# A long convolution followed by phase mixing: first weight loads gated, late operand loads pinned ahead, operand copies split between two issuing engines, PSUM banks reordered

## The chip, the cores and the metric

The kernel runs on one core of one Trainium2 chip. The metric is the device time of one execution in microseconds, and medians over several executions are quoted. The kernel before had run three times when the prediction was written: median 2134.66 us (2131.06 to 2136.18).

## The reference, cut to what matters

```python
def _attn_ref(x, h):                       # x: (8, 5696, 128), h: (5696, 128)
    L = 2 * S
    Yf = np.fft.rfft(x, n=L, axis=1) * np.fft.rfft(h, n=L, axis=0)[None]
    return np.fft.irfft(Yf, n=L, axis=1)[:, :S, :]

def _moe_ref(x, w_theta, w_tok_r, w_tok_i, w_ch):   # x is the result above
    theta = x @ w_theta
    zr, zi = x * np.cos(theta), x * np.sin(theta)
    y = einsum('ts,bsd->btd', w_tok_r, zr) + einsum('ts,bsd->btd', w_tok_i, zi)
    u = x + y
    return u + np.maximum(u @ w_ch, 0.0)
```

A long convolution comes first. Then each token's value is turned by a phase ("phases"), and two 5696 x 5696 matrices W mix the tokens. The mixing is nearly all of the work.

## The kernel before

The convolution runs in stages a to d. Its last stages make `yt` (channels on partitions). A phase step takes one tile of 128 tokens: PE transposes it, PE makes theta, ACT makes sine and cosine, and DVE multiplies (the "zz products"). 22 steps for the first half of the columns ("first series") are woven into stages c and d. 22 for the second half ("second series") are woven into the first products with W. The results must end up, in another layout, in eleven operand tiles b0 to b10. For some tiles they go by "direct copies" from the product in SBUF straight into the b tile. For b9 and b10 (the "late" ones) they go through HBM (`z_hbm`).

The direct copies in the phase step, where some go to Pool (GpSimd) and the rest to SP (SyncE):

```python
            zz = (fh.tile([P, 2, HD * CK], F16, tag="hs", name="zz").bitcast(BF16) if k < 4 else
                  sides["phases"]["zz"].tile([P, 2, 512], BF16, tag="zz", name="zz"))
            zr, zi = zz[:, 0], zz[:, 1]
        ...
        zi_eng.tensor_mul(zi, red, yflat)
        nc.vector.tensor_mul(zr, mag, yflat)
        ...
            if tags is None and j in home:
                for r in range(2):
                    (nc.gpsimd if r and (e or zz_n[0] % 2) else nc.sync).dma_start(
                        home[j][32 * i:32 * i + 32, :4096]...[:, :, q_, r],
                        zz[e * 64 + r:e * 64 + 64:2])
            elif tags is None:
                nc.sync.dma_start(z_hbm[:, p_, j, q_, i].rearrange("z t n -> t z n"), zz[rows])
```

The W loads go into a ring of six slots, four DMAs of 32 partitions to a slot, all issued by Pool. `pump` issues as many as the ring and the limit `upto` allow. `open_ring` starts it:

```python
    def load_w(a, row0, p, j0, nj, ng=4):
        n = ring["n"] % 6
        ring["n"] += 1
        wb = ring["all"][:, n * WB // 6:(n + 1) * WB // 6].rearrange("p (g j) -> p g j", g=4)
        for i in range(4):
            nc.gpsimd.dma_start(
                wb[32 * i:32 * i + 32, :ng, :nj * 64],
                bass.AP(tensor=a.tensor, ...))
        return wb
```

The second series and the first visit to W are woven like this (`i == 1` is the second stretch; `product` is two matmuls of line 974):

```python
        if i == 1:
            for q, (h, s) in enumerate(((0, 0), (0, 1), (1, 0), (1, 1))):
                for n in range(4):
                    for j in range(TJ):
                        product((held, a)[s], s * TJ + j, j, n, (h,))
                        if (n * TJ + j) % 2:
                            next_steps(1)          # one phase step of the second series
                    if n % 2 and q == 1:
                        ring["upto"] += 1
                        pump()
                    if q == 3 and n == 0:
                        ring["upto"] = len(queue)
                        nxt = prepare(2)
            continue
```

The late operands, their loads, the last rows of `ya` (input of the second series), and the first background phases, which load `yT` and `yy` on SP as well:

```python
    def load_b(p, j, pool, eng=nc.scalar):
        t_ = tile_b(p, j, pool)
        for z in range(2):
            eng.dma_start(t_[...], z_hbm[z, p, j]...)
    ...
    def load_ya1(yt=None):
        ...
            for e in range(2):
                nc.sync.dma_start(st[1][HD:, 2 + e, :],
                                  yt[64 * e:64 * e + 64].rearrange("p m n -> p (m n)")[:, :H])
    ...
        if (p, tt, j0 + s0) == (0, 1, 0):
            spread[0][0]()
            spread[1][0]()
    ...
        if first_of_pair:
            ms = [mps.tile([P, 512], F32, tag=f"m{q}", name=f"m{q}") for q in (... (M3, M5, M1, M7))]
```

## Time and profile before

| | before |
|---|---|
| median of three executions | 2134.66 us |
| profiled span | 2137.7 us |
| first matmul of the last stage c (line 323) | 402.4 us |
| first transpose of the second series | 459.5 us |
| last theta of the second series | 515.5 us |
| end of the first visit to W | 546.1 us |
| end of the second visit | 585.6 us |

The last five rows are landmarks read from the timeline of PE. They cut the stretch that the change touches into stages. The prediction below shows the lines of the page that say where the time goes. Two more views are needed later. The first is Pool's timeline at the end of the second series (start, length, engine, line, what it wrote from what, count, and in brackets the idle time before and what ended it):

```profile
512.04 1.10 POOL L436 DMA_DIRECT2D b<-zz  x2 [1.86 <-DVE zz L423]
513.13 1.66 POOL L498 DMA_DIRECT2D ring<-in_moe_w_tok_r_dram  x3
514.75 2.18 POOL L498 DMA_DIRECT2D ring<-in_moe_w_tok_i_dram  x4
516.89 0.61 POOL L572 DMA_DIRECT2D y_hbm<-ring  x1
518.95 0.55 POOL L436 DMA_DIRECT2D b<-zz  x1 [1.45 <-DVE zz L423]
```

The second is the view of SP's waits between 500 and 535 us (total, times, longest):

```profile
SPq L730 <- ACT ring L729: 6.3, 1, 6.3
```

This is the store of a background phase that holds SP's queue for 6.3 us, with the loads of b9 and b10 behind it.

### The profile page before, as it was taken

How to read it: one execution, taken by the hardware profiler on the slowest of the kernel's cores; microseconds unless marked ns; L12 is line 12 of the kernel's file. 1: busy time of each engine (PE TensorE's matmuls, PEld its weight loads, DVE VectorE, ACT ScalarE, POOL GpSimd, SP SyncE). 2: the span in 40 equal slices, each digit the busy share in tenths (PEclk: the TensorE clock that was granted, in tenths of full speed). 3: DMA queues.
4: the chain of work that ended last, by engine and by line, in shares of the span. 5: the costliest groups of instructions: out<-in, count | busy, mean ns of one | idle time of the engine just before them, and what ended most of it. 6: DMA issues, size and time to landing. Idle time of an engine off the chain costs nothing.

```text
span 2137.7 us, 41292 instructions
## 1 busy us (share of the span) xinstructions
PE 1996.2 (93%) x15586; PEld 1123.7 (53%) x15765; DVE 1594.6 (75%) x2880; ACT 675.3 (32%) x997; POOL 898.5 (42%) x1643
## 2 busy tenths in 40 slices
PE   4788889778999999999999998999999999999998
PEld 3787888654444444444444443444444444444444
DVE  7767767677678888888886757577776768686867
ACT  5777877785223333233310000011111111111111
POOL 5301010227345545454557543444545454545451
PEclk8688889899999999999999999999999999999999
DMA  7357474889889998998999879687879797969794
GB/s 145 96 126 169 120 171 112 224 245 230 168 147 180 172 187 157 177 172 178 174 174 153 148 133 277 101 143 131 154 128 158 126 156 127 157 122 159 127 153 90
DMA packets 408839, 334.95 MB, mean 157 GB/s; under 512 B 85927, under 2 KB 359207, under 8 KB 407655
## 3 DMA queue, kind: packets, MB, share of 16 engines
q0 software_dynamic: 225568, 155.93, 51.9%
q1 hardware_dynamic: 177088, 164.84, 27.0%
q10 hardware_dynamic: 5984, 11.54, 1.5%
q8 instruction: 123, 2.02, 0.4%
q14 instruction: 76, 0.62, 0.1%
HBM read 377.11 MB, written 92.49 MB: 220 GB/s over the span
## 4 chain that ended last, share of the span: by engine, by line
PE 64%; DVE 3%; DMA 3%; issue 1%; POOL 1%; ACT 0%; DVEq 0%; ACTq 0%
PE m L1052 57%; PE m L974 2%; DMA b<-z_hbm 2%; DVE c L1059 1%; PE v L786 1%; PE utp L779 1%; PE m L1056 1%; DVE wt L699 1%; PE m L931 1%; POOL ring L498 1%; PE m L929 1%; PE theta_ps L388 0%; PE tpz L727 0%; DMA yT<-yt_hbm 0%; DMA wl<-in_moe_w_tok_i_dram 0%
## 5 line engine op out<-in xcount | busy, mean ns | idle before, releaser
L498 POOL DMA_DIRECT2D ring<-in_moe_w_tok_i_dram x720 | 388.0, 547 | 691.1 <-DVE wt L699 613.4
L498 POOL DMA_DIRECT2D ring<-in_moe_w_tok_r_dram x720 | 386.9, 547 | 151.4 <-DVE wt L699 87.5
L699 DVE STREAM_TRANSPOSE wt<-ring 128x384 f32<-128x384 f32 (+2 forms) x720 | 360.3, 528 | 113.9 <-PE m L1052 70.4
L1052 PE MATMUL m<-b,wt 128*128 128x512 bf16 x1598 | 383.8, 379 | 4.2 <-DVE wt L699 1.7
L1052 PEld LDWEIGHTS <-wt 128*128 128x128 bf16 x1804 | 176.1, 98 | 215.8 <-DVE wt L699 4.4
L1059 DVE TENSOR_TENSOR c<-c,m 128x512 f32<-128x512 f32 x412 | 267.4, 676 | 0.4 <-PE m L1052 0.4
L781 ACT ACTIVATE ring<-utp 128x512 bf16<-128x512 bf16 (+1 forms) x86 | 50.9, 592 | 608.7 <-PE utp L779 608.7
L323 PE MATMUL ps<-r_u,u_t 128*128 128x128 f16 x1024 | 132.8, 229 | 14.1 <-DVE u_t L307 12.6
L324 PE MATMUL ps<-r_v,v_t 128*128 128x128 f16 x1024 | 131.9, 229 | 0.1
L974 PE MATMUL m<-b,wt 128*128 128x512 bf16 x469 | 112.8, 386 | 12.2 <-DMA b<-zz 5.8
L776 ACT ACTIVATE ub<-c 128x512 bf16<-128x512 f32 (+1 forms) x90 | 56.3, 628 | 198.9 <-DVE c L945 117.3
L129 POOL DMA_DIRECT2D x<-in_x_dram x64 | 33.9, 536 | 193.8 <-PE ps L193 181.6
L323 PEld LDWEIGHTS <-u_t 128*128 128x128 f16 x1024 | 106.6, 104 | 15.7 <-DVE u_t L307 15.7
L324 PEld LDWEIGHTS <-v_t 128*128 128x128 f16 x1024 | 105.7, 103 | 2.7 <-DVE v_t L307 1.3
L307 DVE TENSOR_TENSOR u_t<-xs,hs 128x1024 f16<-128x1024 f16 x96 | 71.1, 741 | 38.9 <-ACT xs L305 23.8
L305 ACT ACTIVATE xs<-ps 128x1024 f16<-128x1024 f32 x96 | 94.6, 1014 | 15.3 <-DVE v_t L307 8.8
L193 PE MATMUL ps<-f_t,x 89*128 89x180 f16 x512 | 82.1, 316 | 9.7 <-ACT xs L305 7.5
L974 PEld LDWEIGHTS <-wt 128*128 128x128 bf16 x528 | 51.2, 100 | 67.0 <-issue 12.7
L211 PEld LDWEIGHTS <-w_t 64*128 64x128 f16 x3240 | 63.6, 105 | 37.2 <-issue 23.1
L193 PEld LDWEIGHTS <-x 89*128 89x128 f16 x512 | 73.5, 232 | 12.0 <-issue 11.3
L390 ACT ACTIVATE red<-theta_ps,magic 128x512 f32<-128x512 f32 (+1 forms) x46 | 31.6, 687 | 135.9 <-PE theta_ps L388 105.1
L729 ACT ACTIVATE ring<-tpz 128x512 bf16<-128x512 bf16 (+1 forms) x46 | 27.4, 597 | 144.1 <-PE tpz L727 126.9
(2888 smaller groups left out, 3867.2 us busy)
## 6 DMA issues: line engine op xcount, KB each, us to landing
ring<-in_moe_w_tok_r_dram POOLq DMA_DIRECT2D x352, 96.0 KB, 4.6
ring<-in_moe_w_tok_i_dram POOLq DMA_DIRECT2D x352, 96.0 KB, 4.9
ring<-in_moe_w_tok_r_dram POOLq DMA_DIRECT2D x352, 80.0 KB, 4.5
ring<-in_moe_w_tok_i_dram POOLq DMA_DIRECT2D x352, 80.0 KB, 3.8
hs<-hf_hbm SPq DMA_DIRECT2D x192, 128.0 KB, 3.2
cp_hbm<-c SPq DMA_DIRECT2D x88, 256.0 KB, 2.5
c<-cp_hbm SPq DMA_DIRECT2D x88, 256.0 KB, 4.5
out_dram<-c SPq DMA_DIRECT2D x88, 256.0 KB, 4.2
```

Of the source, the lines that this page charges most:

```text
L193: nc.tensor.matmul(ps[:, i // 2, (i % 2) * 2 * K1:(i % 2 + 1) * 2 * K1], lhs(q + i), f1_t[:NB], start=True, stop=True)
L211: nc.tensor.matmul(ps[:, e, j * HD:(j + 1) * HD], w_t2[rows, c0 + j, N2 * (1 - ri):N2 * (3 - ri)], a_st["a"][rows, ri * K1 + c0 + j, :], s ...
L305: nc.scalar.activation(xs[:, :, :, :ck], ps, AF.Copy)
L307: nc.vector.tensor_tensor(uv[r][:, :, :, c0:c0 + ck], xs[:, :, :, :ck], hv[:, r:r + 1, :, :ck].to_broadcast([P, 2, HD, ck]), op=mult)
L323: nc.tensor.matmul(o, u_t[:, at:at + P], r_u, start=True, stop=False)
L324: nc.tensor.matmul(o, v_t[:, at:at + P], r_v, start=False, stop=True)
L498: nc.gpsimd.dma_start(wb[32 * i:32 * i + 32, :ng, :nj * 64], bass.AP(tensor=a.tensor, offset=a.offset + row0 * S + p * H + i * QR + j0 * 6 ...
L699: nc.vector.transpose(wt.rearrange("p j t r -> p (j t r)").bitcast(F32).rearrange("p (j g t) -> p g j t", j=TJ, g=4)[:, :ng, :nj], wb[:, : ...
L776: nc.scalar.activation(ub[:m].rearrange("p b d -> p (b d)"), c[:m], AF.Copy)
L974: nc.tensor.matmul(ms[n // 2 * 2 + h], a[n][:, j, :, r], bts_of[p][jj][n % 2 * 2 + h][:, r, :], start=(n % 2 == 0 and jj == 0 and r == 0), ...
L1052: nc.tensor.matmul(ms[q], a[q][:, j, :, r], bts[jj][q][:, r, :], start=(jj == 0 and r == 0), stop=(jj == NJ - 1 and r == 1 and q not in left))
L1059: nc.vector.tensor_tensor(c, z, ms[q], op=op)
```

## The change

It has four parts, each with its own intent. (1) Each of the first six W slots is first touched by a one-element Pool copy that reads a zz product, so that the W loads wait until the phases are under way and don't compete with the last loads of `h`. (2) The four PSUM banks of the first products are taken before the first steps of the second series, so that those steps fall on the oldest convolution banks. (3) Every second direct copy goes to Pool: SP has 36 instead of 48, Pool 36 instead of 24. (4) The background loads on SP are put after the loads of b9 and b10.

```diff
@@ phase step
             zr, zi = zz[:, 0], zz[:, 1]
+            sides["zz"] = zz
...
-                    (nc.gpsimd if r and (e or zz_n[0] % 2) else nc.sync).dma_start(
+                    (nc.gpsimd if r else nc.sync).dma_start(
@@ load_w
+        if ring["n"] <= 6:
+            nc.gpsimd.tensor_copy(wb[0:1, 0, 0:1], sides["zz"][0:1, 0, 0:1])
         for i in range(4):
             nc.gpsimd.dma_start(
@@ load_b
-            eng.dma_start(
+            sides["late"] = eng.dma_start(
@@ main loop
                 nxt = prepare(0)
+                ms = [mps.tile([P, 512], F32, tag=f"m{q}", name=f"m{q}") for q in (M3, M5, M1, M7)]
                 next_steps(2)
         if (p, tt, j0 + s0) == (0, 1, 0):
-            spread[0][0]()
-            spread[1][0]()
+            with tc.issue_after(sides["late"].ins):
+                spread[0][0]()
+                spread[1][0]()
...                      (ms is no longer taken here for the first pair; and the addends and
                          first phases of the first two visits stand in the same issue_after)
```

More of the change, by code (lines that the diff above doesn't have):

```diff
@@ L948 @@
         classic = plain(p, tt)
+        if first_of_pair and i:
+            ms = [mps.tile([P, 512], F32, tag=f"m{q}", name=f"m{q}") for q in (range(7) if not classic else (M7, M5, M1, M3) if p else (M2, M6, M1, M7))]
         if first_of_pair:
-            ms = [mps.tile([P, 512], F32, tag=f"m{q}", name=f"m{q}") for q in (range(7) if not classic else (M7, M5, M1, M3) if p else (M2, M6, M1, M7) if tt else (M3, M5, M1, M7))]
             where = ((tt, 1), (22 + tt, 0), (tt, 0), (22 + tt, 1))
@@ L956 @@
         if j0 + s0 == (3 if classic else 2) * TJ:
-            cs = [addend(p, n, t, h) for n, (t, h) in enumerate(where)]
+            with tc.issue_after(sides["late"].ins) if p == 0 and tt == 0 else ExitStack():
+                cs = [addend(p, n, t, h) for n, (t, h) in enumerate(where)]
         def aside(first_of, second_of):
@@ L963, in aside @@
                 _, first, second = spread.pop(0)
-                first()
-                if len(spread) > 1:
-                    spread[1][0]()
+                with tc.issue_after(sides["late"].ins) if p == 0 and tt == 1 else ExitStack():
+                    first()
+                    if len(spread) > 1:
+                        spread[1][0]()
             if second_of and second is not None:
```

## The prediction

> **What bounds the kernel now.** I read the page first: busy time by engine, then the 40 slices. They separate a start that is not bound by PE from a long rest that is.
>
> ```profile
> PE 1996.2 (93%) x15586; PEld 1123.7 (53%) x15765; DVE 1594.6 (75%) x2880; ACT 675.3 (32%) x997; POOL 898.5 (42%) x1643
> ...
> PE   4788889778999999999999998999999999999998
> ...
> PEclk8688889899999999999999999999999999999999
> ```
>
> PE is short of 90% in slices 1 to 10 only (53 us each; to about 550 us). The table by stretch puts numbers on it: busy us of PE, PEld, DVE, ACT, POOL, then granted clock, DMA share and GB/s.
>
> ```profile
> 395.00:400.00 5.00, 0.00 (x0) 0.00 (x0) 1.72 (x3) 1.46 (x3) 3.97 (x8) 0.50 0.98 183
> ...
> 482.00:513.00 31.00, 25.09 (x226) 15.76 (x228) 24.61 (x46) 23.76 (x40) 23.68 (x44) 1.00 0.97 251
> ...
> 529.00:541.00 12.00, 6.89 (x27) 2.96 (x26) 8.12 (x15) 0.83 (x2) 3.75 (x7) 0.72 1.04 270
> ...
> 800.00:900.00 100.00, 99.26 (x504) 46.94 (x513) 83.59 (x164) 33.58 (x54) 51.46 (x96) 1.00 0.93 169
> ```
>
> After 550 us PE is over 99% busy at full clock, and nothing there can be gained by moving loads. The change acts between 390 and 545 us, where convolution ends, the phases run and the first matmuls with W start. So I listed PE's waits in 380 to 560 us (total, times, longest) and found each in the timeline of PE (start, length, idle before it and what ended it).
>
> ```profile
> PE ps L323 <- DVE u_t L307: 7.5, 1, 7.5
> PE m L974 <- DMA b<-zz: 5.8, 3, 3.5
> PE m L974 <- DMA b<-z_hbm: 5.3, 2, 4.9
> PE tpz L566 <- ACT red L411: 3.8, 1, 3.8
> ...
> PE tpz L566 <- DVE ring L571: 2.1, 2, 1.6
> PE tpz L566 <- DMA ya<-yt: 1.6, 1, 1.6
> ```
> ```profile
> 402.41 0.29 PE L323 MATMUL ps<-r_u,u_t 128*128 128x128 f16 x1 [7.50 <-DVE u_t L307]
> ...
> 459.45 0.48 PE L566 MATMUL tpz<-ident_bf,ya 128*128 128x128 bf16 x3 [3.76 <-ACT red L411]
> 461.56 0.29 PE L566 MATMUL tpz<-ident_bf,ya 128*128 128x128 bf16 x1 [1.64 <-DMA ya<-yt]
> ...
> 494.15 0.82 PE L974 MATMUL m<-b,wt 128*128 128x512 bf16 x2 [1.32 <-DMA b<-zz]
> ...
> 513.24 0.42 PE L974 MATMUL m<-b,wt 128*128 128x512 bf16 x1 [3.54 <-DMA b<-zz]
> ...
> 536.70 1.01 PE L974 MATMUL m<-b,wt 128*128 128x512 bf16 x2 [4.89 <-DMA b<-z_hbm]
> ```
>
> The six add up to 26 us. PE runs at half clock after four of them (5.1 us after 402.4, 4.6 after 461.5, 2.7 after 513.2, 3.3 after 536.7: half of that, 8 us, is lost). So 34 us, 1.6% of 2134.66, is the ceiling, and a gain over 2% is nearly excluded from the start.
>
> The timelines of Pool and of SP show who is late:
>
> ```profile
> 392.49 2.18 POOL L498 DMA_DIRECT2D ring<-in_moe_w_tok_r_dram  x4 [14.98 <-PE ps L211]
> ```
> ```profile
> 482.86 8.33 SPq L436 DMA_DIRECT2D b<-zz  x11
> ...
> 495.12 17.04 SPq L436 DMA_DIRECT2D b<-zz  x22
> ...
> 529.26 2.47 SPq L625 DMA_DIRECT2D b<-z_hbm  x4
> ```
>
> SP issues copies without a pause from 482.9 to 512.2, at 17.04 / 22 = 0.77 us each. It lags its products: the 18th zz product of the second phase series is done at 504.5, but its copy to b5, 19th of the 22, issues near 495.12 + 18 x 0.77 = 509.0 and lands 4.1 us later (median), which is 513.1: PE's 3.54 us wait. Pool's line is the start of the first W loads, in the 7.5 us wait's run-up.
>
> **What the Trainium skill says.** "DMA: Bandwidth & Descriptors", Issuing engines are not separate DMA queues: DMAs from SP, ACT and Pool run on the same 16 engines; several issuers save only the issuing time. The trace agrees that bytes share: DMA share is 0.97 in 482 to 513 us. But issue was the limit of SP there, so moving copies can pay once. "PSUM — Partial Sum Buffer", Engine vs sequencer instructions: matmuls start and complete in program order. The trace agrees: transpose b=3 stuck at 461.56 holds all later PE work. "TensorE: Matmul & The Clock Gate", Part 1: after an idle window of about 3.4 us the clock halves until PE was busy about as long. The trace agrees: clock 0.50 in 395 to 400 us, and 128-column matmuls 107 ns apart from 402.8 to 407.5, then 55 ns. So a wait over 3 us also costs about half of the next 3 to 5 us.
>
> **The change, part by part.** I compared the built instruction streams. DVE's is the same. On PE 196 of 15767 matmuls lie in another order, on ACT 7 instructions; on Pool a stretch of 102 becomes 120, on SP one of 76 becomes 64. Everything from the third W visit on is identical.
>
> (1) Gate on the first W loads: six one-element Pool copies from a zz product into partition 0 of a ring slot. Each slot is filled by four DMAs of 32 partitions, and only the first overlaps the written element. In the built stream the other 18 of the 24 stand ungated at the old place; just 6 wait for products. Pool keeps only 8 DMAs in flight (each names the semaphore of the eighth before it). In 392.5 to 402 us Pool issued 14 W loads; 18 ungated ones fill that time as before. The last h load (up to 8.4 us to landing against a median of 3.6) meets the same traffic. Gain: 0 of the 7.5 + 2.0 us. The six late loads come about 418 to 435 us, needed at 457.5: no cost. The copies are negligible beside 0.55 us per DMA issue.
>
> (2) Phase banks: the four m banks are now taken first, so the phases land on the older convolution banks. The built stream drops the ACT wait of the first transposes, so three of four start 3.7 us earlier. The fourth needs the last half of ya, issued by SP at 456.40 and landed at 461.5, in unchanged order. PE idles to 461.5 as before. Gain: 0 to 0.3 us.
>
> (3) Copies half on Pool: SP goes from 48 to 36 direct copies, Pool from 24 to 36. Per phase step SP needs 2 x 0.77 = 1.5 us of a step of 1.97 us, so its lag goes: b5's half is issued near 505 and lands by 509. Pool needs 3 x 0.555 = 1.7 us a step plus 16 W loads; its 78 DMAs from 471.3 us to the last copy (66 before) take 43 us bare, 48 with the waits for landing it had (2.9 us at 483 to 486 among them). So Pool becomes the laggard, and b1's second half may still hold PE near 494. But the built PE order now puts some 26 matmuls of b6 to b8 (5.6 us at 0.216) ahead of Pool's half of b5. Gain: 3.54 us and 1.3 us of half clock after it; the 1.32 and 0.92 us waits half gone (1.1); a later y2 store stretches the 2.1 us wait for DVE ring by 1. Net 4.9 us.
>
> (4) b9 and b10 loads pinned ahead on SP: they no longer stand behind a store that waits for ACT (529.26). b9 can issue near 515 to 517 and lands within 8.0 us, before PE asks at about 526. b10 overlies the zz buffers and waits for Pool's last copy, issued about 519 (8 W loads stand before it), landed 523; b10 lands near 529 to 530, PE asks at 527. So 4.89 + 0.22 becomes about 2.5 us with the half clock (1.7 us) mostly kept; the 0.68 us wait for ACT goes. The background phases only move behind: same work. Net 3.3 us, less 1 for DMA traffic I can't time.
>
> Sum: 0 + 0.1 + 4.9 + 2.3 = about 7 us. 2134.66 - 7 = 2127.7.
>
> **Rivals.** Pool takes SP's place altogether: it sat idle only about 7.3 us in 482 to 513, and 12 more copies ask 6.7. Then waits at 476, 494 and b8 grow by what SP saves: 2132 to 2137. For it: Pool's waits for landing; against: PE's new order. The gate works after all, because fewer W loads overlap the h loads: 7 us more and 2 us of half clock, 2119. Against it: the built stream. Everything works, only the waits for u_t and at the first transposes stay: 26.1 - 7.5 - 3.8 - 1.6 = 13 us, with 3 us of half clock 16 us gained, 2119. Against it: b10's dependence on Pool. A clock that behaves otherwise moves all by 2 us; the three runs before span 5 us.
>
> **Range and chances.** Ends: the second rival and its like (2119 to 2121), and Pool as full substitute with noise (2136). Eight in ten: 2120 to 2135. Faster by 2% needs 42 us, more than all idle time here: 1%. Slower by 2% needs new waits of 43 us in a stretch of 150 us: 1%. Within 2%: 98%.
>
> **What would show it.** Right: PE still waits 6 us or more for u_t near 402; first transposes without an ACT wait but the fourth still on ya near 461; no wait for zz above 2 us near 509 to 513; SP pauses between copies, Pool hardly; b9 issued before 520; one wait for b10 of 1 to 4 us. Wrong: the u_t wait gone (gate), waits of 3 us and more on Pool's copies or on the y2 stores (step 3), b10 later than 533 (step 4), or a change after 600 us, where the streams agree.

## More of the kernel before

In the kernel before, Pool's last copy waits for its product (DVE zz): Pool is ready before the data are. A burst of W loads stands ahead of this copy, but here it delays nothing, because the last product is not done until 518.65 us.

## The result, and the profile after

The changed kernel took 2129.57 us, the median of four executions (2126.97 to 2130.14). The kernel before, executed beside it, took 2134.43 (2131.06 to 2136.18). The ratio is 0.9977 with a 95% interval of 0.9959 to 0.9994. Ratios here are the mean time of one kernel's fast runs over that of the other's fast runs of the same rounds, so they are not quite the ratio of the medians quoted. The predicted time was 2127.7 in a range of 2120 to 2135, and within 2% was given 98%: the number holds. The trace, however, does not show the time coming from where the prediction had it come from.

The page first: busy time by engine, then two rows of the 40 slices.

```profile
PE 1991.5 (94%) x15587; PEld 1119.4 (53%) x15765; DVE 1594.2 (75%) x2880; ACT 675.2 (32%) x997; POOL 908.3 (43%) x1661
...
PE   4788899887999999999999998999999999999998
...
PEclk8698889999999999999999999999999999999999
```

The shape is the same. Pool has 18 more instructions (the six gate copies and twelve direct copies) and 10 us more busy time. The table by stretch (busy PE, PEld, DVE, ACT and Pool, granted clock, DMA share, GB/s):

```profile
482.00:513.00 31.00, 26.77 (x194) 14.67 (x194) 19.60 (x37) 16.48 (x28) 26.58 (x49) 1.00 0.97 246
...
800.00:900.00 100.00, 99.47 (x504) 46.80 (x513) 83.61 (x162) 32.37 (x52) 47.94 (x90) 1.00 0.93 170
```

The late part is as it was (99.47 against 99.26 us of PE in 800 to 900 us). In 482 to 513 us Pool is now busy 26.58 us instead of 23.68; the changed kernel is some 10 us further on in its work at that time, so the two rows don't show quite the same steps. Then PE's waits in 380 to 560 us, and the same waits in PE's timeline:

```profile
PE m L982 <- DMA b<-zz: 7.3, 3, 6.1
PE ps L323 <- DVE u_t L307: 3.8, 1, 3.8
PE tpz L569 <- DMA ya<-yt: 3.3, 1, 3.3
...
PE m L1025 <- DMA yy<-y_hbm: 2.2, 1, 2.2
PE tpz L569 <- ACT red L411: 2.1, 1, 2.1
PE m L982 <- DMA b<-z_hbm: 1.8, 3, 0.7
```

```profile
392.99 0.29 PE L323 MATMUL ps<-r_u,u_t 128*128 128x128 f16 x1 [3.77 <-DVE u_t L307]
...
447.70 0.33 PE L569 MATMUL tpz<-ident_bf,ya 128*128 128x128 bf16 x3 [2.09 <-ACT red L411]
451.36 0.29 PE L569 MATMUL tpz<-ident_bf,ya 128*128 128x128 bf16 x1 [3.33 <-DMA ya<-yt]
...
502.00 9.67 PE L982 MATMUL m<-b,wt 128*128 128x512 bf16 x43 [1.48 <-DVE wt L702]
...
517.78 7.34 PE L982 MATMUL m<-b,wt 128*128 128x512 bf16 x24 [6.11 <-DMA b<-zz]
525.78 1.67 PE L982 MATMUL m<-b,wt 128*128 128x512 bf16 x7 [0.67 <-DMA b<-z_hbm]
531.90 0.43 PE L1025 MATMUL m<-yy,ident_bf 128*128 128x512 bf16 x1 [2.23 <-DMA yy<-y_hbm]
```

(Lines of the kernel have moved by a few: 982 is the product that was 974, 569 the transpose that was 566, 1025 the addend that was 1017.) The 3.54 us wait for a copy at 513 and the 4.89 us wait for b10 at 537 are gone. In their place stands one wait of 6.11 us for a copy at 517.8, and a new one of 2.23 us for an addend, `yy`. Pool's timeline shows why the copy was late:

```profile
505.13 1.07 POOL L437 DMA_DIRECT2D b<-zz  x2
506.19 2.20 POOL L501 DMA_DIRECT2D ring<-in_moe_w_tok_r_dram  x4
508.36 2.18 POOL L501 DMA_DIRECT2D ring<-in_moe_w_tok_i_dram  x4
510.63 0.58 POOL L575 DMA_DIRECT2D y_hbm<-ring  x1
513.16 0.55 POOL L437 DMA_DIRECT2D b<-zz  x1 [1.95 <-DMA ring<-in_moe_w_tok_r_dram]
515.33 0.53 POOL L437 DMA_DIRECT2D b<-zz  x1 [1.62 <-DMA ring<-in_moe_w_tok_r_dram]
```

The last zz product was done at 505.0 us (DVE's timeline: it starts at 504.33 and takes 0.69). Its two copies on Pool were issued at 513.16 and 515.33, because eight W loads, a store and two waits for earlier W loads to land stand before them. (Such waits are the program's own: as the prediction notes, it lets Pool keep only eight DMAs in flight.) In the kernel before, the same burst stood there, but the copy waited for its product in any case. SP was hit as well. Its waits and its timeline:

```profile
SPq L628 <- DMA b<-zz: 10.3, 1, 10.3
```

```profile
501.48 4.81 SPq L437 DMA_DIRECT2D b<-zz  x4
506.46 12.60 SPq L628 DMA_DIRECT2D b<-z_hbm  x4
519.17 0.41 SPq L814 DMA_DIRECT2D yy<-y_hbm  x1
```

The pin worked: the first load of b9 goes out at 506.46. But b10 overlies the buffers of the zz products, so its load waits 10.3 us for Pool's last copies, and the addends `yy` stand behind it until 519.17.

The landmarks make the sum. The stage columns are differences in us:

| | before | after | difference |
|---|---|---|---|
| first W load issued | 392.5 | 388.3 | -4.2 |
| from there to the first stage c matmul | 9.9 | 4.7 | -5.2 |
| stage c to the first transpose of series 2 | 57.0 | 54.7 | -2.3 |
| transpose to the last theta of series 2 | 56.0 | 51.4 | -4.7 |
| last theta to the end of the first visit | 30.6 | 37.3 | +6.7 |
| second visit | 39.5 | 40.2 | +0.7 |
| from there to the end of the span | 1552.1 | 1548.3 | -3.8 |
| profiled span | 2137.7 | 2124.9 | -12.8 |

The profiled executions differ by 12.8 us, far more than the medians. 4.2 of these arise before the first W load. 3.8 arise after the second visit, where the built instruction streams of the two kernels are the same. 5.2 arise between the first W load and the first stage c matmul; 3.7 of these are the wait for `u_t` at line 323, and the experiments will show that this wait varies as much without any change. What the change surely touches, from the first stage c matmul to the end of the first visit, took 143.7 us before and 143.4 after. The phases gain 7 us and the tail after them gives 6.7 back. The second visit is at least 0.7 us longer in every kernel with part 4: 12 small matmuls of background phases, which stood in the tail of the first visit before, have moved into it. The stretch flatters such kernels by that much.

### The profile page after: what moved, and what is told of

It is laid out like the page before. It is cut to its first block, busy times and chain, and to the rows that moved or that the text cites. A ratio compares the mean times of both kernels' runs of the same rounds, so it can differ in the third digit from the quotient of the medians.

```text
span 2124.9 us, 41308 instructions
## 1 busy us (share of the span) xinstructions
PE 1991.5 (94%) x15587; PEld 1119.4 (53%) x15765; DVE 1594.2 (75%) x2880; ACT 675.2 (32%) x997; POOL 908.3 (43%) x1661
## 4 chain that ended last, share of the span: by engine, by line
PE 65%; DMA 2%; DVE 2%; issue 1%; POOL 1%; ACT 0%; DVEq 0%; ACTq 0%; POOLq 0%
PE m L1060 59%; PE m L982 2%; DMA b<-z_hbm 2%; DVE c L1067 1%; PE v L789 1%; PE utp L782 1%; PE m L1064 1%; DVE wt L702 1%; POOL ring L501 1%; PE m L936 0%; PE m L934 0%; PE theta_ps L388 0%; PE tpz L730 0%; DMA wl<-in_moe_w_tok_i_dram 0%; DMA y_hbm<-ring 0%
## 5 line engine op out<-in xcount | busy, mean ns | idle before, releaser
L982 PEld LDWEIGHTS <-wt 128*128 128x128 bf16 x528 | 51.1, 100 | 72.4 <-issue 18.5
```

Source lines behind the costliest of these rows:

```text
L982: nc.tensor.matmul(ms[n // 2 * 2 + h], a[n][:, j, :, r], bts_of[p][jj][n % 2 * 2 + h][:, r, :], start=(n % 2 == 0 and jj == 0 and r == 0), ...
```

## The experiments

Each kernel ran with a profile and in timed rounds beside the kernel before, in three groups of four, each group on one chip. "Stretch" is the time from the first stage c matmul to the end of the first visit, read from the one profiled execution. How well it repeats is known from one repetition only (e5).

| run | median us (runs) | before, beside it | ratio, 95% interval | stretch us |
|---|---|---|---|---|
| changed, first measured | 2129.57 (4) | 2134.43 | 0.9977, 0.9959 to 0.9994 | 143.4 |
| e1 gate only | 2133.83 (5) | 2129.77 | 1.0017, 1.0001 to 1.0032 | 145.0 |
| e2 copies only | 2128.84 (5) | 2129.77 | 0.9996, 0.9982 to 1.0011 | 142.2 |
| e3 pin only | 2127.12 (5) | 2129.77 | 0.9984, 0.9969 to 1.0000 | 135.1 |
| e4 full gate | 2128.41 (5) | 2129.77 | 0.9987, 0.9971 to 1.0002 | 141.4 |
| e5 changed again | 2130.32 (5) | 2129.81 | 1.0008, 0.9996 to 1.0020 | 144.0 |
| e6 changed, without the copies | 2124.34 (6) | 2129.81 | 0.9977, 0.9965 to 0.9990 | 137.8 |
| e7 changed, last copies on SP | 2128.62 (6) | 2129.81 | 0.9998, 0.9985 to 1.0011 | 137.3 |
| e8 changed, last ya loads on Pool | 2127.25 (5) | 2129.81 | 0.9988, 0.9976 to 1.0000 | 143.2 |
| e9 changed, W burst later | 2125.89 (5) | 2131.34 | 0.9985, 0.9971 to 0.9999 | 139.3 |
| e10 pin, banks, ya on Pool | 2129.99 (6) | 2131.34 | 0.9990, 0.9969 to 1.0011 | 138.2 |
| e11 e9 with ya on Pool | 2124.27 (5) | 2131.34 | 0.9974, 0.9960 to 0.9988 | 134.3 |
| e12 e10 with the W burst later | 2128.23 (6) | 2131.34 | 0.9993, 0.9978 to 1.0008 | 140.2 |

All results were correct. All are "same" at the 2% mark; the question is what a few tenths of a per cent are made of. One thing should be seen before anything else: in the first measurement the kernel before took 2134.43 us, and in the three groups 2129.77, 2129.81 and 2131.34. So most of the 5 us that the changed kernel gained at first is a slow group of executions of the kernel before, whatever made it slow.

### e1: the gate alone

```diff
 (before)
+            sides["zz"] = zz
+        if ring["n"] <= 6:
+            nc.gpsimd.tensor_copy(wb[0:1, 0, 0:1], sides["zz"][0:1, 0, 0:1])
```

> The kernel before with the gate alone. Theory P (the prediction's step 1): only the first of each slot's four loads is gated, so Pool's first 10 us of W loads are as dense as before; PE still waits 6 to 9 us for u_t near 400, time within 1.5 us of before (ratio 0.9993 to 1.0007). Rival G (the profile after shows that wait at 3.8 us): the gate thins the loads enough; the wait is 3 to 5 us and the time 4 to 6 us less (ratio 0.997 to 0.998).

Measured: ratio 1.0017. The wait for `u_t` was 4.7 us, against 7.5 in the profile before; the stretch was 145.0 against 143.7. Both theories missed: the wait is shorter than theory P expected, and the time did not fall as rival G expected. The gate alone brings no time; that it costs some is less than what e5 below shows to be the spread between measurements. The shorter wait is not evidence for it: e3, which has no gate at all, has 4.0 us there.

### e2: the copies alone

```diff
 (before)
-                    (nc.gpsimd if r and (e or zz_n[0] % 2) else nc.sync).dma_start(
+                    (nc.gpsimd if r else nc.sync).dma_start(
```

> The kernel before with the direct copies half on Pool and nothing else. Theory P (step 3): SP's lag goes, the 3.5 us wait for b<-zz near 513 falls under 1.5 us, time 3 to 5 us less. Rival S (Pool takes SP's place): waits for Pool's copies of 3 us or more appear, at 490 to 525 us, time within 2 us of before.

Measured: ratio 0.9996. The second series indeed ran faster (49.7 us from its first transpose to its last theta, against 56.0), and the time from there to the end of the visit grew from 30.6 to 35.8 us. So most of the 6.3 us was paid back at once: in waits of 2.79 us for a copy and of 2.09 and 3.43 us for b9 and b10, all near the end of the visit. The 3 to 5 us of time that theory P expected did not come.

### e3: the pin alone

```diff
 (before)
-            eng.dma_start(
+            sides["late"] = eng.dma_start(
...
+            with tc.issue_after(sides["late"].ins):
                 spread[0][0]()
                 spread[1][0]()
...                      (the other issue_after blocks of the change as well)
```

> The kernel before with the b9 and b10 loads pinned ahead of the later loads on SP. Theory P (step 4): the 4.9 us wait for b<-z_hbm near 537 falls to 1 to 3 us, time 2 to 4 us less. Rival S: the load is then held by the last zz copies instead, the wait only moves, and the time is within 1 us of before.

Measured: ratio 0.9984, which is 3.4 us less (4.6 by the means over all runs). The stretch shrank by 8.6 us to 135.1, the largest effect of any single part. 5.8 of these lie in the tail after the last theta, where the pin acts, and 0.7 come back in the second visit. In PE's timeline the two waits for DMA of more than 1 us after 500 us are these:

```profile
501.41 0.38 PE L977 MATMUL m<-b,wt 128*128 128x512 bf16 x1 [2.83 <-DMA b<-zz]
...
525.12 0.38 PE L1020 MATMUL m<-yy,ident_bf 128*128 128x512 bf16 x1 [1.62 <-DMA yy<-y_hbm]
```

SP's timeline shows both late loads going out back to back:

```profile
503.20 4.56 SPq L436 DMA_DIRECT2D b<-zz  x5
507.87 2.49 SPq L625 DMA_DIRECT2D b<-z_hbm  x4
512.18 0.33 SPq L811 DMA_DIRECT2D yy<-y_hbm  x1
```

With the old split of copies nothing held b10: in the view of waits SP spends 0.4 us on a store and 0.3 on PE ahead of these four loads, and no more. PE's wait for b10 is gone (0.5 us in all for operands from HBM). This is the number to compare with the 10.3 us that the same load waited in the changed kernel.

### e4: the changed kernel with a gate that holds all W loads

```diff
 (changed)
-            nc.gpsimd.tensor_copy(wb[0:1, 0, 0:1], sides["zz"][0:1, 0, 0:1])
+            nc.gpsimd.tensor_copy(wb[:, 0, 0:1], sides["zz"][:, 0, 0:1])
```

> The changed kernel with the gate copy over all 128 partitions, so that all 24 W loads are gated and not 6. Theory P: the W loads now start after the first gated products (near 410), the wait for u_t near 400 falls from the 3.8 us of the profile after to under 1.5 us, time 3 to 6 us below the changed kernel, so 8 to 11 us below before (ratio 0.995 to 0.9963). Rival G: the partial gate had taken what there was to take; within 1 us of the changed kernel (ratio near 0.9977). Rival L: the W loads come too late for the first transposes near 450 and collide with the b loads; slower than the changed kernel.

The gate as written writes partition 0 only, so of each slot's four DMAs just the first must wait. Here all do. Pool's timeline (the first W load of this kernel):

```profile
410.55 0.49 POOL L499 COPY ring<-zz 128x1 bf16<-128x1 bf16 x1 [37.62 <-DVE zz L424]
411.34 2.20 POOL L501 DMA_DIRECT2D ring<-in_moe_w_tok_r_dram  x4 [0.30 <-POOL ring L499]
```

and PE's timeline at the wait that the gate is meant for:

```profile
393.25 0.29 PE L323 MATMUL ps<-r_u,u_t 128*128 128x128 f16 x1 [2.90 <-DVE u_t L307]
```

Measured: ratio 0.9987. With no W load in flight before 411 us PE still waits 2.9 us, where theory P expected under 1.5. That is the shortest of all fourteen traces, and the nearest thing to a floor of this wait that they show. So of the 7.5 us in the kernel before at most 4.6 could belong to W traffic. But ungated kernels show 7.5 (before), 6.4 (e2), 4.0 (e3), 6.0 (e10) and 3.9 (e12), and partly gated ones 3.8, 4.7, 6.8, 5.2, 4.6, 4.6, 4.4 and 6.4: the two sets lie on top of each other. The full gate is the only one outside, by 0.9 us, in one trace. PE's wait for the last copies was 8.15 us here, the longest of all; whether the later W loads have to do with it is not shown. Part 1 as written does nothing that these runs can see, and why the wait varies between 3.8 and 7.5 us stays open.

### e5: the changed kernel again, unaltered

```diff
 (changed; no edit)
```

> The changed kernel once more, unaltered. Theory J (jitter): the profile of the kernel before happened to be a late one; from the first stage-c matmul (402.4 in it) to the end of the first W visit (546.1) before took 143.7 us and the changed kernel 143.4, and the times of one kernel spread by 4 us, so the true gain is small: ratio 0.997 to 1.0, that stretch again 141 to 145 us. Rival P (the prediction): 5 to 7 us, ratio 0.9965 to 0.998, and the stretch 5 us shorter than before's.

Measured: ratio 1.0008, 0.9996 to 1.0020. The first measurement had 0.9977, 0.9959 to 0.9994. These intervals don't even touch, though the kernel is the same. Either the chip or chance decides more than the change, and a 95% interval from one chip's rounds is too narrow as a statement about the kernel. The stages of the trace, on the other hand, repeat well: 54.8, 51.1, 38.1 and 40.2 us against 54.7, 51.4, 37.3 and 40.2, and a stretch of 144.0 against 143.4, while the two profiled spans differ by 7.6 us. So do the two telling lines, here from the view of SP's waits of this run:

```profile
SPq L628 <- DMA b<-zz: 10.3, 1, 10.3
```

and from PE's timeline:

```profile
522.24 8.92 PE L982 MATMUL m<-b,wt 128*128 128x512 bf16 x31 [4.68 <-DMA b<-zz]
...
535.89 0.38 PE L1025 MATMUL m<-yy,ident_bf 128*128 128x512 bf16 x1 [2.47 <-DMA yy<-y_hbm]
```

From here on stages are what the argument rests on, with the times as a check. The long wait for a copy itself is less steady than the stretch: 6.11 us in the first trace and 4.68 here.

### e6: the changed kernel without part 3

```diff
 (changed)
-                    (nc.gpsimd if r else nc.sync).dma_start(
+                    (nc.gpsimd if r and (e or zz_n[0] % 2) else nc.sync).dma_start(
```

> The changed kernel with the direct copies split as before (the other three parts stay). Theory S (Pool takes SP's place): the copies part costs more than it saves in the presence of the pinned loads, since Pool's last copies stand behind eight W loads; without it the 6.1 us wait for b<-zz near 518 falls under 4 us, the stretch is 133 to 138 us, and the time is 3 to 6 us less than the changed kernel's. Theory P (step 3, a net gain of 4.9 us from the copies): 3 to 5 us more than the changed kernel's.

Measured: ratio 0.9977, and on the same chip in the same rounds a mean of 2125.67 us against 2131.41 for e5: 5.7 us less without the copies. The stretch is 6.2 us shorter (137.8 against 144.0). The series is slower (57.1 us against 51.1) and the tail much shorter (25.2 against 38.1). The longest wait for a copy is shorter too:

```profile
508.70 0.38 PE L982 MATMUL m<-b,wt 128*128 128x512 bf16 x1 [3.72 <-DMA b<-zz]
```

This is the clearest pair, since time and trace agree: in company with the other parts, the new split of the copies costs about what the prediction had it gain.

### e7: the changed kernel with the last step's copies on SP

```diff
 (changed)
-                    (nc.gpsimd if r else nc.sync).dma_start(
+                    (nc.gpsimd if r and ti != 20 else nc.sync).dma_start(
```

> The changed kernel with the copies of the last phase step alone all on SP. Theory S: the wait near 518 is only those two copies behind eight W loads on Pool; it falls from 6.1 us to under 2.5, the b10 load starts some 4 to 8 us earlier, the stretch falls to 134 to 138 us and the time by 4 to 7 us against the changed kernel. Rival C: the wait is DMA bandwidth (share 0.97 there); the copies land as late from SP, within 2 us of the changed kernel.

Only the copies of the last step move, out from behind the W loads. PE's timeline in the place where the changed kernel waited 6.11 us:

```profile
504.16 16.97 PE L982 MATMUL m<-b,wt 128*128 128x512 bf16 x69 [2.26 <-DVE wt L702]
521.79 1.89 PE L982 MATMUL m<-b,wt 128*128 128x512 bf16 x7 [0.66 <-DMA b<-z_hbm]
```

69 products run without a wait. SP's wait for the load of b10 fell from 10.3 to 0.9 us:

```profile
SPq L628 <- DMA b<-zz: 0.9, 1, 0.9
```

The stretch is 137.3 us, 6.7 less than e5. The copies landed in time from SP, so the rival that blames DMA bandwidth fails. This shows the cause of the late copy: its place behind the W loads in Pool's queue. The time follows only in part (mean 2129.30 against 2131.41 of e5, ratio 0.9998 to before), less than the 4 to 7 us expected. 2.8 us of what is missing are in the trace: the second visit took 43.0 us instead of 40.2. Whether this belongs to the edit, one trace does not tell.

### e8: the changed kernel with the last ya loads on Pool

```diff
 (changed, load_ya1)
-                nc.sync.dma_start(st[1][HD:, 2 + e, :],
+                nc.gpsimd.dma_start(st[1][HD:, 2 + e, :],
```

> The changed kernel with the two last loads of ya issued by Pool, which is idle there (15 us before 441.85), and not by SP. Theory P (step 2): the bank change is hidden by the fourth transpose's wait for ya; with ya earlier the waits at the first transposes (2.1 for ACT and 3.3 for ya) fall to under 2.5 us together and PE stays at full clock or nearly so; the stretch is 2 to 5 us shorter than the changed kernel's. Rival A: ACT's last copy of yt comes at 451.6 less the 10 us that this profile is earlier, and the load itself takes 5 us, so only 0 to 1.5 us come of it.

This is aimed at the wait that hides what part 2 brings: the fourth first transpose waits 3.3 us for the last half of `ya`, queued on SP. PE's timeline:

```profile
447.65 0.71 PE L569 MATMUL tpz<-ident_bf,ya 128*128 128x128 bf16 x4 [2.09 <-ACT red L411]
455.68 1.01 PE L982 MATMUL m<-b,wt 128*128 128x512 bf16 x2 [3.81 <-DMA b<-z_hbm]
```

All four transposes now run together, so that wait is gone. But 7 us later PE waits 3.81 us for the first operands from HBM, and the stretch is 143.2, as before the edit. A wait on one load has turned into a wait on another: Pool issues the first of these operand loads 59.0 us after the first stage c matmul here (at 451.84) and 59.1 us after it in the changed kernel (at 452.07), so starting the transposes earlier only made PE wait there. The other three kernels with this edit (e10, e11, e12) wait 3.0 to 3.9 us at the same place. The 2 to 5 us expected of the stretch did not come; rival A was nearer. Ratio 0.9988; by its mean it is 4.3 us faster than e5, which the stretch doesn't explain.

### e9: the changed kernel with the W burst after the last phase step

```diff
 (changed)
                     if q == 3 and n == 0:
-                        ring["upto"] = len(queue)
                         nxt = prepare(2)
+                    if q == 3 and n == 1:
+                        ring["upto"] = len(queue)
+                        pump()
```

> The changed kernel with one edit: the eight W loads that Pool issues ahead of the copies of the last phase step are released after that step. Theory S (Pool's last copies stand behind those loads and their landings): Pool issues them within 2 us of the last zz product instead of 8 to 10, the wait for b<-zz of 4.7 to 6.1 us near 518 falls under 1.5, and the stretch from the first stage-c matmul to the end of the first W visit falls from 143.4 and 144.0 us to 133 to 138; time 4 to 8 us less than the changed kernel's. Rival C (DMA bandwidth): wait and stretch stay within 2 us. Rival D: the next W loads come too late and the wait for wt grows by as much.

This keeps part 3 whole and takes the W loads out of the way instead. Pool's timeline:

```profile
504.84 1.07 POOL L437 DMA_DIRECT2D b<-zz  x2
505.91 2.20 POOL L501 DMA_DIRECT2D ring<-in_moe_w_tok_r_dram  x4
```

Now the last two copies go first and the W loads behind them. PE's wait at this place fell to 2.01 us:

```profile
511.50 10.06 PE L982 MATMUL m<-b,wt 128*128 128x512 bf16 x37 [2.01 <-DMA b<-zz]
...
524.72 0.38 PE L1027 MATMUL m<-yy,ident_bf 128*128 128x512 bf16 x1 [2.51 <-DMA yy<-y_hbm]
```

The stretch is 139.3 us and the ratio to before 0.9985. Together with e7 this settles the cause from two sides: move the copies or move the loads, and most of the wait goes. Some 2 us stay, and both figures miss the expectation a little (a wait under 1.5, a stretch of 133 to 138). Pool's own backlog of copies and stores is the likely rest: the last product was done at 502.84 us, and its copies went out at 504.84 and 505.38 without a W load between. Rival D fails: after the later burst PE has no wait for W products (wt) in the first visit. The changed kernel was not run on this chip, so the 4 to 8 us of time expected against it is not tested.

### e10, e11 and e12: putting the better parts together

e10 is the kernel before with pin, banks and the ya loads on Pool, without gate and new split:

```diff
 (before)
+            sides["late"] = eng.dma_start(        ... and the issue_after blocks of the change
+                ms = [mps.tile(...) for q in (M3, M5, M1, M7)]
-                nc.sync.dma_start(st[1][HD:, 2 + e, :],
+                nc.gpsimd.dma_start(st[1][HD:, 2 + e, :],
```

> The kernel before with the pinned loads, the bank order and ya's last loads on Pool; no gate, copies split as before. If the pin is the part that pays (stretch 135.1 alone) and the banks pay once ya is early, the stretch is 131 to 135 us, the wait for ya is gone, time 4 to 8 us less than before (ratio 0.996 to 0.998). If the banks and ya give nothing, the stretch is 135 to 138 and the ratio 0.998 to 0.999.

e11 is the changed kernel with the edits of e8 and e9 both; e12 is e10 with the edit of e9:

```diff
 (e11: changed)
-                nc.sync.dma_start(st[1][HD:, 2 + e, :],
+                nc.gpsimd.dma_start(st[1][HD:, 2 + e, :],
...
-                        ring["upto"] = len(queue)
...
+                    if q == 3 and n == 1:
+                        ring["upto"] = len(queue)
+                        pump()
```

> The changed kernel with both edits, W loads after the last step and ya's last loads on Pool. If the copies on Pool are good by themselves (the phases took 51.1 us against 56.0 and 57.1) and only their tail was bad, this is the best of all: stretch 128 to 133 us, ratio 0.993 to 0.996. If Pool is short of time in general, stretch 135 or more and not better than the pinned kernel with banks and ya.

```diff
 (e12: e10)
-                        ring["upto"] = len(queue)
...
+                    if q == 3 and n == 1:
+                        ring["upto"] = len(queue)
+                        pump()
```

> The pinned kernel with banks, ya on Pool and W loads after the last step, copies split as before, so without Pool's extra copies. Its last copies are SP's, which no W load precedes: the W edit should give nothing here, within 2 us of the same kernel without it. If it is clearly better than that, W loads matter by their traffic and not by their place on Pool.

Measured: e11 has the shortest stretch of all (134.3 us) and the lowest ratio, 0.9974 (0.9960 to 0.9988): mean 2124.76 us against 2130.37 of the kernel before. Both fall short of what was expected (128 to 133 us, 0.993 to 0.996). It is the best version found, but its lead over e9, e3 and e6 lies within what e5 has shown chips or chance to do. e10 and e12 have 0.9990 and 0.9993, less than their stretches of 138.2 and 140.2 suggest; e10 had been expected at 131 to 135 us. With the old split of copies, moving the W burst brings nothing: the wait for a copy is 3.8 us in e10 and 3.9 in e12, and SP, which has its 48 copies back, is again the one that issues without a pause ahead of it (22 copies in 16.32 us in e10), as in the kernel before.

e11 and e12 differ in the gate and in the split of the copies alone, and they ran on the same chip. The one with the new split has a stretch 5.9 us shorter and a mean 4.0 us lower. The gate by itself had brought nothing (e1), so this suggests that the new split does gain about what was predicted once its last copies are out from behind the W burst. e7 against e6, the other such pair, does not show it (137.3 against 137.8 us), so it stays open.

## Why the prediction was right or wrong, point by point

The number was right, in part by luck, and the reasons were right only in part. A sum of four terms came out near because one was too large and another too small, and because it was taken from a base of 2134.66 us, higher than the median of any later group, so that the first measurement fell on a good side.

**Step 1, the gate (predicted 0).** Right. That 18 of the 24 first DMAs stay ungated is visible in the trace, where the first W load goes at 388 us and the first gate copy at 411. The check that the prediction offered ("still 6 us or more for u_t") would have misled: the first trace has 3.8, the repetition 6.8. The rival in which the gate works would have read its proof from the first trace. e4 shows that even a gate on everything leaves 2.9 us.

**Step 2, the banks (predicted 0 to 0.3).** Right in size, with one error: the ACT wait did not go, it shrank from 3.8 to 2.1 us in every kernel with the new banks. The wait for `ya` behind it grew from 1.6 to 3.3, and so the gain was masked as foretold. e8 adds what the prediction did not have: with `ya` out of the way a third wait appears behind it, for the first operands from HBM, 3.8 us. To the first transpose 57.0 us became 54.7, but to the fourth, which PE needs as well, 59.2 became only 58.4. The banks alone were never run.

**Step 3, the copies (predicted 4.9 gained).** This is the step that failed, and it is the mis-sized term: alone it brings 1.5 us of stretch (142.2 against 143.7, less than the 2.0 us by which e10 and e12 differ), and beside the other parts it costs about 6 (144.0 in e5 against 137.8 in e6; 5.7 us by the means). SP's lag did go, and the 3.54 us wait with it, as predicted; the series became 4.7 to 6.3 us faster. What was missed is the queue in which the copies then stand. The prediction counted the eight W loads ahead of Pool's last copy, but only as a delay of b10; it did not carry the delay to b8, whose own half is that copy. PE asked for b8 at 511.7 and had it at 517.8. The faster the series ran, the earlier PE arrived there: the gain was turned into this wait. The sign of being wrong that the prediction had set for this step, a wait of 3 us or more on Pool's copies, came true with 6.11 us. The rival "Pool takes SP's place" was right in kind, and had named b8. Its range of 2132 to 2137 was not met in the first measurement; e5's runs (2129.89 to 2134.53) reach into it.

**Step 4, the pin (predicted 3.3, less 1).** The mechanism was right and the size too small: alone the pin shortens the stretch by 8.6 us and the time by 3.4 (by the ratio) to 4.6 us (by the means). In the changed kernel most of that was lost again to step 3, since the load of b10 waited 10.3 us for Pool's last copies, whereas alone it hardly waited. The b10 wait of 1 to 4 us that was predicted came as 0.67 and 0.5, because PE was held at b8 first. A wait had also been missed: PE waits 1.4 to 3.3 us for the addends `yy` in every kernel with the pin except e4 (where it came later through its long wait for a copy), and not at all in the kernel before. It is not shown to be a cost of the pin's order: SP issues these loads right behind b9 and b10 in the kernel before too (531.84 after 529.26), and the copies alone brought such a wait as well (1.2 us in e2). It may only be that PE now arrives earlier.

**The ceiling and the chances.** No run contradicts the ceiling of 34 us, and with it the 98% for "within 2%". Two of its readings are loose: slice 7 is at 9 already, while slices 25 and 40 are at 8; and "over 99% busy after 550 us" does not hold throughout, since PE is busy 17.91 us in 600 to 620 and 18.01 in 620 to 640, 90% of each. The change does not act there. The 1% for slower was as it should be. The range of 15 us held all medians of this document.

**What stays open.** Whether the changed kernel is faster than the kernel before: the first measurement says 0.9977, the second 1.0008. Over the thirteen measurements the difference of the mean time goes along with the stretch only loosely (correlation 0.6 by my calculation from the table and the means). No kernel was run in which only the pin, only the banks or only the gate is taken out of the changed kernel, so what those do inside it is read from its stages and not measured by itself. Why e10 and e12 are slower than their stretches suggest was not found.

## What to carry to other kernels

When copies are moved to a less busy engine, look at what stands in that engine's queue at the moment when the last copies become ready, not at its share of busy time: here a burst of eight loads, which could be issued later without a new wait (e9), stood before two copies that PE and another load were waiting for. Issue what is needed first, first, and release bursts of prefetch after the last urgent transfer, or keep them on another queue (which was not tried here). And when an effect is smaller than the spread between executions, compare lengths of stages in the traces and measure both kernels again, in another group of runs, before believing an interval.

## What the Trainium skill lacked or had wrong

- "DMA: Bandwidth & Descriptors", Issuing engines are not separate DMA queues: it says that several issuers save only the issuing time, usually small beside the transfer. That is not wrong, but the section does not speak of the order within one issuer. Pool spent 4.4 us on issuing eight W loads and then waited 1.95 and 1.62 us for W loads to land, so two copies whose data were ready at 505.0 us went out at 513.2 and 515.3. A copy on Pool takes 0.54 us of issuing and one on SP 0.60 (medians), so 36 to 48 of them are no small matter in a series of 51 to 56 us.
- "DMA: Bandwidth & Descriptors", Anatomy of one DMA — SWDGE (gpsimd) path: its fit of 2.0 us plus the bytes over 436e3 per us gives an estimate of 2.15 us for a copy of 64 KB and 2.2 us for a W load of 96 KB. In the changed kernel between 480 and 530 us Pool's copies took a median of 3.4 us to landing, and its W loads of that size 4.5 and 7.3. The DMA share in that stretch is 1.01, and the section has no landing time for a transfer among so much traffic.
- No page that I found tells how far two measurements of one kernel lie apart: 0.9977 and 1.0008 of the kernel before, with 95% intervals that do not overlap.
